# Gate values of the first chunk: four loads of each replaced by one load and a copy made by TensorE

## The chip, the cores and the metric

The kernel runs on one core of one Trainium2 chip. The metric is the device time of one execution in microseconds (us), and a kernel's time is the median of its runs. A profile is one execution recorded instruction by instruction; its span runs from the first to the last instruction of the program and is a little shorter than the device time.

## The reference

An mLSTM cell and a feed-forward layer follow each other. For each of 4 x 8 pairs of batch and head, over 768 tokens, with head size 40:

```python
m_new = max(f_gate[t] + m, i_gate[t])                 # m starts at -1e30
f_stab, i_stab = exp(f_gate[t] + m - m_new), exp(i_gate[t] - m_new)
C = f_stab * C + i_stab * outer(v[t], k[t]);  n = f_stab * n + i_stab * k[t]
y[t] = sigmoid(o_gate[t]) * (C @ q[t]) / max(abs(n . q[t]), 1)
```

The results are laid out as 3072 tokens of 320 values, x, and then `h = x @ w_in` (320 to 2048), `g = max(0.01 h, h)`, `out = g @ w_out` (2048 to 320). All of it is float32.

## The kernel before

**Tiling.** The sequence is cut into six chunks of 128 tokens. A step is one chunk of one batch, so there are 24 steps, and a chunk has four. Within a chunk the recurrence is written as a masked product: scores q.k are weighted by a matrix w of exponentials of gate sums, and the state carried from earlier chunks is added. The feed-forward layer of a chunk (`ff_units`) runs on TensorE between the cell work of the next chunk. TensorE, VectorE, ScalarE and GpSimd carry out their instructions in the order in which the program lists them (a hand-written order); each DMA queue (SyncE's, and ScalarE's for some loads) also issues in program order. A DMA takes one of eight completion semaphores, so its issue waits for the load that used that semaphore before it.

**Start of the program.** `first_chunk()` (L1169) is a hand-written list. SyncE's queue issues, in this order: the gate i loads, then k, q, v of step 0, k, q, v of step 1, the two o gates, and the first part of w_in; then the loads of steps 2 and 3 and the rest of w_in. ScalarE's queue issues the gate f loads and the gates of chunks 1 and 2.

**Gates of chunk 0.** `gates(0)` (L318) runs on VectorE over tiles f0 and i0, in which the 32 rows (batch and head) by 128 tokens stand four times over, on partitions 0-31, 32-63, 64-95 and 96-127: L109 to L111 load each of the two gates four times. F is the running sum of f (L325), m the running maximum (L329), `a = F - m` (L331) and `bu[:, 0] = i - F` (L333). For chunk 0 `a` lies in the third of three 128-column slots of `early`, an unused stretch of the later activations tile `acts`; the first two slots hold bf16 copies of the identity and of the causal mask, made by GpSimd (L152, L153).

**The spread.** `spread_masks()` (L475) writes the causal mask into four PSUM banks `ab` by four bf16 products of 512 columns (L479). `spread_first()` (L485) then adds a(t) + b(s) for every head: for each it multiplies a one-column pick from the identity, broadcast, with 32 rows of `a` or `bu` (L495). Four such products, one on each group of 32 rows of the array, run beside each other; this is why the gates stand on all four row groups. There are 32 products for `a` and 32 for `bu`, and the profile records each as two instructions. `first_exps()` (L500) turns the banks into w on ScalarE by four instructions (L504).

**What follows on TensorE.** `gates_T(0)` (L369) transposes the gate factors; `u_transpose(0)` (L629) transposes k and q of step 0 by eight products (L635), VectorE copies them out to kqT (L638); `u_scores(0)` (L640) multiplies them (L649) and VectorE multiplies the scores into w (L653). Step 1 follows in the same way, its kqT copied by ScalarE. `warm(6)` (L364, L367) is six products of the identity with itself, whose results nobody reads, issued ahead of the spread.

**After that.** `u_values`, `gate`, `u_x` and `state` finish steps 0 and 1; `narrow_weights` (L278 on) puts loaded weights into their final form on ScalarE (L300, L301) and VectorE (L302 to L309) as they land; L857 is the first feed-forward product. L413 and L522 are GpSimd's copies of v and mask additions for chunk 1, L621 the transposes of its k and q.

Of the kernel before, what the change touches and what calls it, by code (L numbers as in the profile page):

```python
# [9 lines left out]
F32 = mybir.dt.float32  # L10
# [9 lines left out]
def kernel(  # L20
# [26 lines left out]
    nc = tc.nc  # L47
    B, H, S, D = q.shape
    P = 128
    BH = B * H  # L50
# [16 lines left out]
    GT = B * P  # L67
# [13 lines left out]
    wk = ctx.enter_context(tc.tile_pool(name="wk", bufs=2))  # L81
    psf = ctx.enter_context(tc.tile_pool(name="psf", bufs=4, space=PSUM))
    psc = ctx.enter_context(tc.tile_pool(name="psc", bufs=4, space=PSUM))
# [18 lines left out]
    sync, by_act = queues = Ordered(nc.sync), Ordered(nc.scalar)  # L102

    RG = P // BH
    f_all = f_gate.rearrange("b h s -> (b h) s")
    i_all = i_gate.rearrange("b h s -> (b h) s")
    f0 = gp.tile([P, P], F32, name="f0")
    i0 = gp.tile([P, P], F32, name="i0")
    for r in range(RG):  # L109
        nc.scalar.dma_start(f0[ts(r, BH), :], f_all[:, :P])  # L110
        sync.dma_start(i0[ts(r, BH), :], i_all[:, :P])  # L111
    fi = {}

    def load_fi(c):
# [7 lines left out]
    ident = consts.tile([P, P], F32, name="ident")  # L122
# [24 lines left out]
    w_all = consts.tile([P, NL, H * P], F32, name="w")  # L147
    acts = consts.tile([P, NF, GT], F32, name="acts")
    acts_l = acts[:].rearrange("p f t -> p (f t)")
    early = acts_l[:, 5 * GT : 5 * GT + 3 * P].rearrange("p (n t) -> p n t", t=P)  # L150
    identb, cmaskb = (early[:, n, : P // 2].bitcast(BF16) for n in range(2))
    nc.gpsimd.tensor_copy(identb, ident[:])  # L152
    nc.gpsimd.tensor_copy(cmaskb, cmask[:])  # L153
    for n in range(NL):
        nc.vector.memset(kn[:, n, :, D:], 0.0)
        nc.vector.memset(qn[:, n, :, D:], 0.0)
        nc.gpsimd.memset(S_t[n][:, 1, :, D:], 2.0)
        nc.gpsimd.memset(S_t[n][SL:, 0], 0.0)
# [159 lines left out]
    def gates(c):  # L318


        m0 = m0s.get(c)
        n = P if c == 0 else BH
        fc, il = (f0[:], i0[:]) if c == 0 else (fi[c][:, 0, :], fi[c][:, 1, :])
        F = wk.tile([n, P], F32, name="F", bufs=1)
        nc.vector.tensor_tensor_scan(F[:], fc, zeros[:n].to_broadcast([n, P]), 0.0, op0=ALU.add, op1=ALU.add)  # L325
        if c > 0:
            nc.vector.tensor_scalar(il, il, scalar1=m0[:], scalar2=None, op0=ALU.subtract)
        m = wk.tile([n, P], F32, name="m", bufs=1)
        nc.vector.tensor_tensor_scan(m[:], fc, il, -1e30 if c == 0 else 0.0, op0=ALU.add, op1=ALU.max)  # L329
        a = early[:, 2, :] if c == 0 else wk.tile([n, P], F32, name="a", bufs=1)  # L330
        nc.vector.tensor_tensor(a[:], F[:], m[:], op=ALU.subtract)  # L331
        bu = wk.tile([n, 3, P], F32, name="bu", bufs=1)
        nc.vector.tensor_tensor(bu[:, 0, :], il, F[:], op=ALU.subtract)  # L333
        if c + 1 < NB:
            m1 = wk.tile([BH, 1], F32, name="m0")
            if c == 0:
                nc.vector.tensor_copy(m1[:], m[:BH, P - 1 :])
            else:
                nc.vector.tensor_tensor(m1[:], m0[:], m[:, P - 1 :], op=ALU.add)
            m0s[c + 1] = m1  # L340
        if c > 0:
            na = wk.tile([BH, 1], F32, name="na")
            nc.vector.tensor_tensor(na[:], m[:, SL - 1 : SL], F[:, SL - 1 : SL], op=ALU.subtract)
        bus[c] = bu, a, (na if c > 0 else None)
# [19 lines left out]
    def warm(n):  # L364
        t = psf.tile([P, P], F32, name="warm", tag="mm")
        for _ in range(n):
            nc.tensor.matmul(t[:], lhsT=ident[:], rhs=ident[:], start=True, stop=True)  # L367
# [47 lines left out]
    def load_first(s, i):  # L415

        d = st.setdefault(s, {})
        at = 4 * HW * 2 + s * Dm
        dst = (kn[:, s, :, :D], qn[:, s, :, :D], S_t[s][:, 1, :, :D], blocks(raw_l[:, at : at + Dm]))[i]
        d["k"], d["q"], d["va"], d["o"] = kn[:, s], qn[:, s], S_t[s][:, 1], raw_l[:, at : at + Dm]  # L420
        sync.dma_start(dst, (k, q, v, o_gate)[i][s, :, :P, :].rearrange("h p d -> p h d"))
# [43 lines left out]
    def spread_q(s):  # L465
# [4 lines left out]
        for r in range(2):  # L470
            sync.dma_start(
                d["ea"][ts(r, SL)], a_dr[c, 1, 1 - r, b * H : (b + 1) * H, :].partition_broadcast(SL),
            )

    def spread_masks():  # L475

        ab = [psf.tile([P, 2, H // RG, P], F32, name=f"ab{r}", tag="mm") for r in range(RG)]
        for t in ab:
            nc.tensor.matmul(  # L479
                t[:].rearrange("p n m t -> p (n m) t"), lhsT=identb,  # L480
                rhs=cmaskb.unsqueeze(1).to_broadcast([P, 2 * H // RG, P]), start=True, stop=False, skip_group_check=True,
            )
        return ab

    def spread_first(ab, a, bu, s2):  # L485

        for n in range(2):
            st.setdefault(s2 + n, {})["w"] = w_all[:, s2 + n].rearrange("p (h t) -> p h t", t=P)
            for m in range(H // RG):
                for left in (False, True)[: 1 if bu is None else 2]:  # L490
                    for r in range(RG):
                        bh = (s2 + n) * H + m * RG + r
                        rows = ts(r, BH)
                        pick = ident[rows, r * BH + bh : r * BH + bh + 1].to_broadcast([BH, P])
                        nc.tensor.matmul(  # L495
                            ab[r][:, n, m, :], lhsT=bu[rows, 0, :] if left else pick, rhs=pick if left else a[rows, :],
                            start=False, stop=left or bu is None, skip_group_check=True,
                        )

# [129 lines left out]
    def u_transpose(s, copies):  # L629
        d = st[s]  # L630
        d["kqT"] = wk.tile([P, 2, PR * P], F32, name="kqT")
        for i in range(2):
            tp = psc.tile([P, PR, P], F32, name="tkq", tag="c")
            for j in range(PR):
                nc.tensor.transpose(  # L635
                    tp[:, j, :], d["kq"[i]][:, 2 * j : 2 * j + 2, :].rearrange("p h d -> p (h d)"), ident[:],
                )
            copies[i](d["kqT"][:, i], tp[:].rearrange("p j t -> p (j t)"))  # L638
# [530 lines left out]
    def first_chunk():  # L1169

        for n in range(2):
            for i in range(3):
                load_first(n, i)
        for n in range(2):
            load_first(n, 3)
        load_weights(0, (0,))
        on_v, on_s = nc.vector.tensor_copy, nc.scalar.copy
        gates(0)
        gates_exp(0)
        load_fi(2)  # L1180
        warm(6)
        ab = spread_masks()
        bu, a, _ = bus[0]
        spread_first(ab, a, bu, 0)
        gates_T(0, bu)
        prep_vu(0)
        first_exps(ab, 0)
        u_transpose(0, (on_v, on_v))
        u_scores(0)
        u_transpose(1, (on_s, on_s))  # L1190
        ab = spread_masks()
        gates(1)
        u_scores(1)
        prep_vu(1)
        prepare_tiles()
        e = next_exps(ab, 2)
        w, w1 = narrow_weights(0, 0), narrow_weights(0, 1)
        n0, n1 = narrow_weights(1, 0), narrow_weights(1, 1)
        ffs = []
        prep_o(0)  # L1200
        prep_o(1)
        u_values(0)
        gate(0)
        spread_first(ab, a, None, 2)
        u_values(1)
        load_first(2, 0)
        load_first(2, 1)
        load_weights(0, (1,))
        load_first(3, 0)
        load_first(3, 1)  # L1210
        load_first(2, 2)
        load_first(3, 2)
        load_first(2, 3)
        load_first(3, 3)
        load_weights(1, (0,))
        load_weights(1, (1,))
        run(e, 6)
        u_x(0)
        gate(1)
        run(w, 2)  # L1220
        run(w, 4)
        u_x(1)
        state(0)
        state(1)
        state_copy(0)
        state_copy(1)
        prepare_step(0)
        prepare_step(1)
        run(e, 2)
        ffs = ff_units(0)  # L1230
        u_transpose(2, (on_s, on_s))
        run(e, 4)
        gates_exp(1)
        run(w1, 2)
        run(e, 4)
        ffs[0]()
        run(w1, 2)
        prep_vu(2)
        prep_vu(3)
        u_scores(2)  # L1240
        u_transpose(3, (on_v, on_s))
        run(w1, 2)
        u_gates(1)
        u_scores(3)
        prep_o(2)
        prep_o(3)
        u_values(2)
        ffs[1]()
        gate(2)
        u_values(3)  # L1250
        gate(3)
        u_x(2)
        state(2)
        u_x(3)
        state(3)
        state_copy(2)
        run(n0, 4)
        state_copy(3)
        run(n0, 2)
        run(n1, 6)  # L1260
        prepare_step(2)
        prepare_step(3)
        return ffs
# [160 lines left out]
```

## Time and profile before

| | us |
|---|---|
| device time, median of 3 runs (lowest to highest) | 476.22 (475.19 to 476.83) |
| span of the profiled execution | 472.6 |
| TensorE matmul busy | 462.6 |
| VectorE / ScalarE / GpSimd busy | 339.1 / 203.7 / 172.0 |

The device time of the profiled execution alone is not given; its span lies 3.6 us below the median of the runs. In the rows of the profile, PE is TensorE's matmul side and PEld its weight loads, DVE is VectorE, ACT ScalarE, POOL GpSimd, SP SyncE; a q behind a name (SPq, ACTq) is that engine's instruction queue, where DMAs are issued. A row of the timeline has start, duration, engine, source line, operation, out<-in, shapes and count, and in brackets how long the engine had been idle and what ended that. Neighbouring instructions of one kind are merged into one row, and rows of one engine can overlap, since products are pipelined.

### The profile page before, as it was taken

What the parts mean: (1) busy time and instruction counts of PE and PEld (TensorE: products, weight loads), DVE (VectorE), ACT (ScalarE), POOL (GpSimd) and SP (SyncE); (2) the same over time, 40 slices, a digit from 0 to 9 for tenths busy, and PEclk for the clock granted to TensorE, in tenths of its full rate; (3) what the DMA queues carried; (4) which work ended last, traced back from release to release, by engine and by line L of the source; (5) the groups of instructions that cost most, each with busy time, mean ns of one, the idle gap of its engine ahead of it and who ended that gap; (6) DMA issues with size and microseconds to landing.
All of it is one profiled execution on the core that took longest, in us unless ns stands there. A gap on an engine that the chain in (4) does not pass through costs nothing.

```text
span 472.6 us, 14150 instructions
## 1 busy us (share of the span) xinstructions
PE 462.6 (98%) x5729; PEld 417.8 (88%) x5729; DVE 339.1 (72%) x607; ACT 203.7 (43%) x497; POOL 172.0 (36%) x205
## 2 busy tenths in 40 slices
PE   7998999999999999999999999999999999999997
PEld 6787878777788899988999988999988999988997
DVE  3878589999579989878688867788947786105531
ACT  3755888755336511367311366311456311253210
POOL 4340577264335164923214923214822005300020
PEclk9999999999999999999999999999999999999999
DMA  9999988877742594865755764853875203100001
GB/s 117 174 176 183 223 192 229 199 154 159 155 135 56 157 171 107 185 152 115 179 125 108 172 144 120 196 120 76 189 147 122 65 21 81 58 0 2 8 8 42
DMA packets 161281, 59.31 MB, mean 126 GB/s; under 512 B 123904, under 2 KB 152640, under 8 KB 161216
## 3 DMA queue, kind: packets, MB, share of 16 engines
q1 hardware_dynamic: 121088, 51.20, 49.0%
q10 hardware_dynamic: 40128, 7.21, 9.3%
q8 instruction: 45, 0.74, 0.7%
q14 instruction: 20, 0.16, 0.2%
HBM read 51.68 MB, written 6.70 MB: 124 GB/s over the span
## 4 chain that ended last, share of the span: by engine, by line
PE 86%; SPq 6%; DMA 3%; DVE 1%; ACT 1%; issue 1%; POOL 0%; DVEq 0%; ACTq 0%
PE ph L1021 33%; PE po L914 33%; PE po L879 8%; SPq L96 6%; PE pT L796 3%; PE sd L708 3%; PE ph L857 3%; DMA acts<-in_moe_w_in_dram 2%; DMA acts<-in_v_dram 1%; PE sd L714 1%; PE hN L768 1%; PE tk L621 0%; ACT kqT L627 0%; PE tq L606 0%; DVE w_in L308 0%
## 5 line engine op out<-in xcount | busy, mean ns | idle before, releaser
L914 PE MATMUL po<-w_out,acts 128*128 128x160 f32 x640 | 89.1, 300 | 0.0
L914 PEld LDWEIGHTS po<-w_out,acts 128*128 128x128 f32 x640 | 87.3, 190 | 0.6 <-ACT acts L1046 0.3
L1021 PE MATMUL ph<-xT,w_in 64*128 64x256 f32 x720 | 82.7, 378 | 0.0
L1021 PEld LDWEIGHTS ph<-xT,w_in 64*128 64x128 f32 x720 | 69.5, 187 | 8.3 <-issue 0.6
L1050 DVE TENSOR_TENSOR acts<-acts,ph 128x512 f32<-128x512 f32 x60 | 38.4, 682 | 40.4 <-PE ph L1021 40.3
L914 PE MATMUL po<-raw,acts 128*128 128x160 f32 x480 | 66.4, 300 | 0.0
L914 PEld LDWEIGHTS po<-raw,acts 128*128 128x128 f32 x480 | 65.4, 190 | 0.3
L1054 ACT COPY acts<-ph 128x512 f32<-128x512 f32 x60 | 32.2, 588 | 49.5 <-PE ph L1021 49.5
L522 POOL TENSOR_TENSOR w<-w,i 128x512 f32<-128x512 f32 x20 | 31.9, 1603 | 53.2 <-DMA w<-a_dr 22.1
L1046 ACT ACTIVATE acts<-acts 128x1024 f32<-128x1024 f32 x30 | 31.6, 1055 | 40.6 <-DVE acts L1050 32.3
L684 POOL TENSOR_TENSOR S<-S,f 40x336 f32<-40x336 f32 x36 | 31.3, 868 | 46.7 <-PE pT L796 31.1
L530 ACT ACTIVATE w<-w,gT 128x64 f32<-128x64 f32 x160 | 41.6, 337 | 12.3 <-DMA a_dr<-a 5.3
L725 DVE TENSOR_TENSOR qn<-w,sd 64x384 f32<-64x384 f32 (+1 forms) x80 | 33.4, 418 | 13.7 <-ACT acts L1054 7.8
L857 PE MATMUL ph<-xT,w_in 64*128 64x256 f32 x320 | 37.9, 383 | 1.8 <-DVE w_in L309 0.7
L879 PE MATMUL po<-w_out,acts 128*128 128x320 f32 x128 | 36.7, 437 | 0.0
L857 PEld LDWEIGHTS ph<-xT,w_in 64*128 64x128 f32 x320 | 31.5, 187 | 5.8 <-ACT acts L865 1.1
L810 POOL TENSOR_TENSOR xb<-xb,den 128x320 f32<-128x320 f32 x16 | 11.6, 727 | 67.7 <-DVE xb L807 65.4
L1021 PE MATMUL ph<-acts,w 64*128 64x256 f32 x320 | 36.3, 379 | 0.0
L1021 PEld LDWEIGHTS ph<-acts,w 64*128 64x128 f32 x320 | 30.6, 187 | 3.6
L879 PEld LDWEIGHTS po<-w_out,acts 128*128 128x128 f32 x128 | 23.5, 190 | 9.2 <-ACT acts L865 0.3
L595 DVE TENSOR_TENSOR qn<-kqT,ea 64x512 f32<-64x512 f32 x32 | 30.9, 965 | 0.8
L952 POOL TENSOR_TENSOR y<-y,raw 128x160 f32<-128x160 f32 x10 | 9.5, 953 | 59.2 <-ACT y L951 59.2
(181 smaller groups left out, 736.5 us busy)
## 6 DMA issues: line engine op xcount, KB each, us to landing
rb<-in_k_dram SPq DMA_DIRECT2D x64, 80.0 KB
rb<-in_q_dram SPq DMA_DIRECT2D x64, 80.0 KB
rb<-in_o_gate_dram SPq DMA_DIRECT2D x64, 80.0 KB
ea<-a_dr SPq DMA_DIRECT2D x32, 128.0 KB
raw<-in_moe_w_out_dram SPq DMA_DIRECT2D x6, 640.0 KB
w<-a_dr ACTq DMA_DIRECT2D x24, 128.0 KB
x_dr<-x SPq DMA_DIRECT2D x64, 40.0 KB
xT<-x_dr SPq DMA_DIRECT2D x16, 160.0 KB
```

The costliest lines, as they stand in the source:

```text
L522: nc.gpsimd.tensor_tensor(w, w, cm2.unsqueeze(1).to_broadcast([P, H, SL]), op=ALU.add)
L530: yield nc.scalar.activation(w[:, h, :], w[:, h, :], AF.Exp, bias=gT[c][:, 0, bh : bh + 1], scale=1.0)
L595: nc.vector.tensor_tensor(mixed(s)[rows, 1 - r], d["kqT"][rows, 1].rearrange("p (h t) -> p h t", t=SL), d["ea"][rows], op=ALU.mult,)
L684: nc.gpsimd.tensor_tensor(new, old, g, op=ALU.mult)
L725: nc.vector.tensor_tensor(mixed(s)[toks, u, hs], w[toks, hs], bank[1 - u][to[u][hs.start], hs], op=ALU.mult,)
L857: nc.tensor.matmul(ph[r][:, cols], lhsT=w_row(r, slot, j), rhs=xT[DP * r : DP * (r + 1), slot, cols], start=(slot == 0), stop=(slot == KC ...
L879: nc.tensor.matmul(po[n][:], lhsT=acts[:, f, ts(n, P)], rhs=w_out[:, f, :], start=(f == 0), stop=(f == NF - 1),)
L914: nc.tensor.matmul(bank[:], lhsT=left[:, f, :], rhs=right[:, f, :], start=f == 0, stop=f == KH - 1)
L1021: nc.tensor.matmul(bank[r][:, e, :], lhsT=left(r)[rows, e], rhs=right(r)[rows], start=first and e == 0 and m == 0, stop=e == 1 and m == le ...
L1046: nc.scalar.activation(to, z, AF.Prelu, alpha=0.01)
L1050: nc.vector.tensor_tensor(to[:, 2 * r : 2 * r + 2], to[:, 2 * r : 2 * r + 2], bank[r], op=ALU.add)
L1054: nc.scalar.copy(to[:, 2 * r : 2 * r + 2], bank[r])
```

## The change

Each gate of chunk 0 is loaded once, onto partitions 0-31, and `gates(0)` works on 32 rows. GpSimd makes one more tile in `early` (now four slots): on 32 rows, the 32-by-32 identity four times side by side. A new function, `replicate`, multiplies it with `a` and with `bu[:, 0]` on TensorE, which puts both on four row groups in PSUM; one VectorE copy of 128 x 256 brings them to SBUF, where the spread reads them. `u_transpose(0)` moves from behind `first_exps` to ahead of the spread. `warm(6)` becomes `warm(2)`. The second spread, for steps 2 and 3, reads the same copied `a`.

```diff
-    for r in range(RG):
-        nc.scalar.dma_start(f0[ts(r, BH), :], f_all[:, :P])
-        sync.dma_start(i0[ts(r, BH), :], i_all[:, :P])
+    nc.scalar.dma_start(f0[:BH], f_all[:, :P])
+    sync.dma_start(i0[:BH], i_all[:, :P])
...
-    early = acts_l[:, 5 * GT : 5 * GT + 3 * P].rearrange("p (n t) -> p n t", t=P)
+    early = acts_l[:, 5 * GT : 6 * GT].rearrange("p (n t) -> p n t", t=P)
...
     nc.gpsimd.tensor_copy(cmaskb, cmask[:])
+    nc.gpsimd.tensor_copy(early[:BH, 2, :].rearrange("p (r n) -> p r n", r=RG), ident[:BH, :BH].unsqueeze(1).to_broadcast([BH, RG, BH]))
...
-        n = P if c == 0 else BH
-        fc, il = (f0[:], i0[:]) if c == 0 else (fi[c][:, 0, :], fi[c][:, 1, :])
+        n = BH
+        fc, il = (f0[:BH], i0[:BH]) if c == 0 else (fi[c][:, 0, :], fi[c][:, 1, :])
...
-        a = early[:, 2, :] if c == 0 else wk.tile([n, P], F32, name="a", bufs=1)
+        a = wk.tile([n, P], F32, name="a", bufs=1)
...
+    def replicate(a, bu):
+        rows = early[:, 2:]
+        t = psc.tile([P, 2, P], F32, name="rep", tag="c")
+        pick = rows[:BH, 0, :]
+        for n, part in enumerate((a[:], bu[:, 0, :])):
+            nc.tensor.matmul(t[:, n, :], lhsT=pick, rhs=part, start=True, stop=True)
+        nc.vector.tensor_copy(rows, t[:])
+        return rows[:, 0, :], rows[:, 1, :]
...
-                            ab[r][:, n, m, :], lhsT=bu[rows, 0, :] if left else pick, rhs=pick if left else a[rows, :],
+                            ab[r][:, n, m, :], lhsT=bu[rows, :] if left else pick, rhs=pick if left else a[rows, :],
...
-        warm(6)
+        warm(2)
         ab = spread_masks()
         bu, a, _ = bus[0]
-        spread_first(ab, a, bu, 0)
+        a, left = replicate(a, bu)
+        u_transpose(0, (on_v, on_v))
+        spread_first(ab, a, left, 0)
         gates_T(0, bu)
         prep_vu(0)
         first_exps(ab, 0)
-        u_transpose(0, (on_v, on_v))
         u_scores(0)
```

More of the change, by code (lines that the diff above doesn't have):

```diff
@@ L336, in gates @@
             if c == 0:
-                nc.vector.tensor_copy(m1[:], m[:BH, P - 1 :])
+                nc.vector.tensor_copy(m1[:], m[:, P - 1 :])
             else:
```

## The prediction

> **What bounds the kernel now.** I read the page's slices first, then TensorE's busy time in stretches of the start, then the waits there, then the chain of waits. The slices:
>
> ```profile
> PE   7998999999999999999999999999999999999997
> DMA  9999988877742594865755764853875203100001
> ```
>
> TensorE is below nine tenths only in the first slices and the last one; the DMA engines are full in the first five slices, 59 us. Two stretches ahead of 70 us and one behind (start:end, length, then busy time and instruction count of PE, PEld, DVE, ACT, POOL; DMA share and GB/s at the end):
>
> ```profile
> 45.00:50.00 5.00, 3.95 (x91) 3.58 (x93) 4.73 (x12) 4.55 (x8) 2.84 (x3) 1.00 0.83 192
> 65.00:70.00 5.00, 4.04 (x90) 3.31 (x90) 4.86 (x6) 4.93 (x15) 4.78 (x6) 1.00 0.73 174
> 70.00:75.00 5.00, 5.00 (x91) 4.35 (x81) 4.69 (x9) 4.62 (x11) 3.73 (x5) 1.00 0.82 216
> ```
>
> The slices have TensorE full from there to the last one, so this change can be worth only what it takes off the time at which TensorE gets there. What holds it up before that are loads, as the timeline shows:
>
> ```profile
> 42.46 0.78 ACT L865 ACTIVATE acts<-ph 128x256 f32<-128x256 f32 x2 [1.37 <-PE ph L857]
> 45.42 0.80 ACT L300 ACTIVATE w_in<-raw 128x640 f32<-128x640 f32 x1 [2.17 <-DMA raw<-in_moe_w_in_dram]
> 52.41 4.86 PE L857 MATMUL ph<-xT,w_in 64*128 64x256 f32 x40 [0.73 <-ACT acts L865]
> 60.93 1.79 POOL L522 TENSOR_TENSOR w<-w,i 128x512 f32<-128x512 f32 x1 [7.27 <-DMA w<-a_dr]
> ```
>
> ScalarE waits 2.17 us for w_in at 45.42 and is then busy (4.55 of 5 us to 50, all but the end of that wait) until it releases TensorE at 52.41; GpSimd waits 7.27 us for w at 60.93, and TensorE's last gap, between 65 and 70 us, comes behind that. The chain of waits (start, duration, what) follows the first of these loads back through SyncE's queue to the issue of the first big one:
>
> ```profile
> 2.58 0.42 SPq L96
> ...
> 28.96 8.66 DMA acts<-in_moe_w_in_dram
> 37.73 0.80 ACT w_in L300
> ```
>
> So the start is a train of loads in one queue. Its time is when the first big load is issued, plus work that keeps the DMA engines full.
>
> **The change part by part.**
>
> *The loads.* The queue's start now:
>
> ```profile
> 0.75 1.79 SPq L96 DMA_DIRECT2D i<-in_i_gate_dram  x4
> 0.76 1.84 ACTq L110 DMA_DIRECT2D f<-in_f_gate_dram  x4
> 2.58 0.42 SPq L96 DMA_DIRECT2D kn<-in_k_dram  x1
> 3.05 0.58 SPq L96 DMA_DIRECT2D qn<-in_q_dram  x1
> 6.39 1.30 SPq L96 DMA_DIRECT2D S<-in_v_dram  x1
> ```
>
> Three of SyncE's four gate issues go: (2.58 - 0.75) x 3/4 = 1.37 us. k of step 0 is issued at 1.21, and every load behind it moves with it, since by the program nothing in that queue waits for arithmetic in the first 30 us: an issue waits for the load eight before it, and that moves too. ScalarE's own loads, of the gates of chunk 1, move by as much. The six loads also leave the DMA engines. For the first 10 us ScalarE's queue, eight loads of 16 KB, shows the first of these rows (packets, MB, share of 16 engines); the others are stretches:
>
> ```profile
> q10 hardware_dynamic: 384, 0.13, 6.9%
> 1.00:2.00 1.00, 0.53 (x2) 0.53 (x3) 1.00 (x6) 0.00 (x0) 0.96 (x5) 1.00 0.09 26
> 3.00:4.00 1.00, 1.00 (x7) 1.00 (x7) 0.00 (x0) 0.33 (x1) 0.89 (x3) 1.00 0.38 71
> 6.00:7.00 1.00, 1.00 (x17) 0.97 (x20) 0.00 (x0) 0.00 (x0) 0.00 (x0) 1.00 1.53 146
> ```
>
> 0.69 us of all engines, so six loads are 0.5. That is the upper bound of what their absence adds; nothing is the lower, since before 4 us the share is 0.09 to 0.38 against 1.53 when full (shares add up overlapping packets). I take 0.1, near the lower end.
>
> *The gates on 32 rows.* VectorE starts at 4.03, 1.43 us after the last of ScalarE's issues ended (0.76 + 1.84 = 2.60):
>
> ```profile
> 4.03 0.42 DVE L325 TENSOR_TENSOR_SCAN F<-f,zeros 128x128 f32<-128x128 f32 x1 [1.47 <-DMA f<-in_f_gate_dram]
> 13.34 0.41 DVE L325 TENSOR_TENSOR_SCAN F<-fi,zeros 32x128 f32<-32x128 f32 x1
> 5.01 0.28 DVE L333 TENSOR_TENSOR bu<-i,F 128x128 f32<-128x128 f32 x1
> 1.47 2.93 PE L367 MATMUL warm<-ident 128*128 128x128 f32 x12 [1.47 <-POOL ident masks.py:199]
> 4.19 1.91 PE L479 MATMUL ab<-acts 128*128 128x512 bf16 x4
> ```
>
> One issue ends at 1.22, so F starts at 2.65; 32 rows cost what 128 do (0.41 against 0.42). bu was done 5.29 - 4.03 = 1.26 after the start, so a and bu stand at 3.9, not 5.3.
>
> *Two idle products for six.* Twelve records in 2.93 us are 0.24 each; two products end at 2.45, and the four mask products, 1.91, at 4.36. TensorE waits for nothing there: its masks are made ahead of GpSimd's added copy. That copy, 32 x 128, delays only the clearing of tiles that are used later; its price lies between nothing and the 0.72 us of GpSimd's 128 x 320 product (row at 11.96 below), and GpSimd's next work waits for gT, at 9.04, anyway.
>
> *The copy onto four row groups.* Two products are four records at 0.24: 4.36 to 5.34. Then VectorE's 128 x 256 copy out of PSUM; no row has this shape, and the bounds are these two:
>
> ```profile
> 9.04 0.22 DVE L380 COPY gT<-tg 128x64 f32<-128x64 f32 x1 [3.69 <-PE tg L373]
> 9.53 1.29 DVE L638 COPY kqT<-tkq 128x512 f32<-128x512 f32 x2 [0.26 <-PE tkq L635]
> ```
>
> 0.22 to 0.65; by columns 0.4. Below the first it cannot be. It lies beside TensorE's transposes of step 0, and costs nothing there; without them it would be 0.4 on the path.
>
> *The transposes ahead of the spread.* TensorE takes its instructions in order, so the spread, and behind it the exponentials, now wait until k and q of step 0 have landed and eight transposes are through. Rows:
>
> ```profile
> 6.03 0.81 PE L495 MATMUL ab<-acts,ident 32*128 32x128 f32 x8
> 6.62 0.65 PE L495 MATMUL ab<-ident,bu 32*128 32x128 f32 x8
> 7.05 0.65 PE L495 MATMUL ab<-acts,ident 32*128 32x128 f32 x8
> 7.76 0.39 PE L495 MATMUL ab<-acts,ident 32*128 32x128 f32 x8
> 7.98 0.39 PE L495 MATMUL ab<-ident,bu 32*128 32x128 f32 x8
> 8.85 2.06 ACT L504 ACTIVATE w<-ab 128x512 f32<-128x512 f32 x4 [3.12 <-PE tg L373]
> 11.96 0.72 POOL L540 TENSOR_TENSOR vu<-S,gT 128x320 f32<-128x320 f32 x1 [1.64 <-DMA S<-in_v_dram]
> 12.13 1.28 DVE L653 TENSOR_TENSOR w<-w,sc 128x512 f32<-128x512 f32 x2 [1.32 <-PE sc L649]
> 12.66 1.07 ACT L638 COPY kqT<-tkq 128x512 f32<-128x512 f32 x2 [1.75 <-PE tkq L635]
> ```
>
> The groups of the spread begin 0.43 us apart (6.62, 7.05) and later 0.22 (7.76, 7.98): TensorE goes from half speed to full near 7.5, though the view's granted clock says 1.00 there. At half speed eight transposes at 0.24 last from 5.34 to 7.3. The landing of q has no row; bounds: the gate's load took 1.43 + 0.46 = 1.9 us from its issue, v of step 1, with the queue full, 11.96 - 6.39 = 5.6. Issued at 1.68, q lands between 3.6 and 7.3; by its place, second of six, near 5. TensorE wants it at 6.3; at the late bound the spread comes 1 us later. So the spread starts at 7.3, not 6.03, has one slow group and seven fast, and ends at 9.3, not 8.65: 0.6 late. The exponentials run from 9.45 to 11.5. But the eight transposes behind the spread are gone, and kqT is copied long before: scores run from 9.5 to 10.6, VectorE starts on w when the third exponential ends, 9.45 + 1.55 = 11.0, not 12.13, and ScalarE copies step 1's kqT at 11.5, not 12.66. Arithmetic is **1.1 us earlier** from there. GpSimd's scaling of v, behind gT, comes some 0.6 later than now; only the state products at the end of steps 0 and 1 read it.
>
> **Sum.** Loads 1.37 + 0.1, arithmetic 1.1 earlier. ScalarE was free at 43.25 and waited until 45.42, so for its gain the loads decide, and they pass 1.47 on to 52.41 and, through the w load at 60.93, to 70. The span becomes 472.6 - 1.5 = 471.1. The median of the runs shown lies 3.6 above the profiled span; with the same 3.6 the time is **474.7**, 0.32% less.
>
> **The rivals.**
>
> *Arithmetic comes late* (ends above). With loads 1.37 earlier ScalarE's free time ahead of 45.42 is 2.17 - 1.37 = 0.8 us, if arithmetic has not moved. If it is x us later than now, the gain is 1.37 - (x - 0.8): nothing at x = 2.17, a loss beyond. The mechanism is half speed on TensorE that lasts longer because four idle products are gone and the products are fewer. If it lasts until step 1's scores are done (now at 15.0): the spread takes 7.3 to 10.75. Step 1's scores follow in the trace at
>
> ```profile
> 10.87 1.16 PE L649 MATMUL sc<-kqT 40*128 40x128 f32 x16 [0.94 <-DVE kqT L638]
> 13.85 1.16 PE L649 MATMUL sc<-kqT 40*128 40x128 f32 x16
> ```
>
> From the spread's end at 8.65 to 15.0 are 6.35 us, less the 0.94 idle and 1.0 of step 0's transposes 4.4 of work; at half speed 8.8, so the scores end at 19.5, x = 4.5, and the loss is 2.3: **478.5**. It decides where half speed lasts beyond about 15 us (x = 2.17). Against it: TensorE is as continuously busy as now, from 1.47 to 9.3. For it: the slow state is seen to last 6 us after the first product. The Trainium skill's "TensorE: Matmul & The Clock Gate", Part 1, says that the array runs at half rate until about 3.4 us of a free-running window have been busy, since the default is the throttled state; this speaks against taking products out. By that rule idle products at the start buy full speed. The trace agrees on two speeds, groups 0.43 and 0.22 apart. By the page's figure one window more would end at an estimated 10.9, and the spread's slow groups would then cost about 1.5 us: x = 0.4, within ScalarE's 0.8, and the sum would stay.
>
> *Arithmetic takes part of the gain*: q lands late or the clock rises late, x between 1 and 2: gains of 1.2 to 0.2, about **475.5**.
>
> *The change does not do what it says*: the DMA engines, not the issues, pace the first loads, so that issuing earlier moves nothing, **476.2**. Against it: the shares of 0.09 to 0.38 above.
>
> **How the numbers follow.** I give the forecast 0.73; late arithmetic 0.14; partial 0.08; nothing 0.05. The forecast's own range is 473.6 to 475.6: 0.5 more for the six loads' DMA time, 0.9 less if waits further on give some back, and the 0.4 or so by which runs differ. A change of 0.3%, 1.43 us, is about what a measurement of this kernel tells from none; the forecast lies just beyond it (474.79), so of its 0.73 I give 0.52 to faster and 0.21 to within. The partial case and the one of nothing are within; of the late one 0.12 is slower, 0.02 within. Faster 0.52, within 0.36, slower 0.12. The range 473.5 to 477.0 holds forecast, partial and nothing and leaves out most of the late case.
>
> **What would show it.** SyncE issues k at 1.2; ScalarE's waits at 37.7 and 45.4 end 1.4 earlier; TensorE starts its product at 51.0, not 52.41; VectorE's first w product starts near 11.0; the spread near 7.3, with groups 0.22 apart soon after. Groups still 0.43 apart at the end of the spread would point to the clock; a spread held beyond 7.5 by a wait for q, to the load; waits at 45.4 that have not moved, to DMA engines that set the pace. The forecast is wrong, too, if TensorE has new gaps after 70.

## The result and the profile after

The changed kernel takes **474.30 us** (median of 18 runs, 472.69 to 475.71) against 475.47 (18 runs, 474.52 to 477.68) for the kernel before. The ratio is 0.997 with a 95% interval of 0.9959 to 0.998: faster, by about as much as the 0.3% that was taken as the bound of what can be told. 474.7 had been predicted.

Two corrections of the scale come first. With 18 runs the median of before is 475.47, not the 476.22 of the first three. And every run of the changed kernel lists its device time 1.8 us above its span (474.27 and 472.5 in the profiled one). The span of 472.6 shown of before thus belongs to a run of about 474.4, one of its quickest. The two profiled spans, 472.6 and 472.5, differ by nothing; the medians differ by 1.17. So where the gain lies has to be read stage by stage.

The slices of the changed kernel (page, part 2):

```profile
PE   8999989999999999999999999999999999999997
DMA  9999978878752695865755765753774203100001
```

TensorE still has its low slices ahead of 70 us only. Three stretches, with the same columns as those shown of before:

```profile
45.00:50.00 5.00, 5.00 (x102) 4.51 (x104) 4.73 (x11) 4.91 (x12) 4.58 (x5) 1.00 0.94 195
65.00:70.00 5.00, 3.76 (x116) 3.02 (x114) 4.79 (x5) 4.89 (x17) 4.25 (x5) 1.00 0.56 148
70.00:75.00 5.00, 5.00 (x77) 4.26 (x77) 4.71 (x9) 4.04 (x10) 2.48 (x5) 1.00 0.73 193
```

TensorE is busy for all of 45 to 50 us, where it was for 3.95 of 5. The gap between 65 and 70 is still there. What TensorE waited for between 20 and 72 us, first before, then after (us in all, times, longest):

```profile
PE tk L621 <- DMA kn<-in_k_dram: 1.1, 1, 1.1
PE sd L714 <- POOL vu L550: 1.0, 1, 1.0
PE ph L857 <- DVE w_in L309: 0.7, 1, 0.7
PE ph L857 <- ACT acts L865: 0.7, 1, 0.7
PE xt L845 <- DVE x L756: 0.5, 1, 0.5
PE ph L857 <- DVE S L672: 0.4, 1, 0.4
```

```profile
PE sd L724 <- POOL vu L560: 1.1, 1, 1.1
PE ph L867 <- DVE w_in L309: 0.8, 1, 0.8
PE xt L855 <- DVE x L766: 0.5, 1, 0.5
PE tg L373 <- DVE w L663: 0.3, 1, 0.3
```

4.4 us before, 2.7 after: the waits for k of a later step, for ScalarE at 52.41 and for the state are gone. (Lines of the program are 10 higher behind the new function.) The rows that answer to those of the prediction, in the order of the timeline:

```profile
43.14 0.80 ACT L300 ACTIVATE w_in<-raw 128x640 f32<-128x640 f32 x1
...
45.94 9.31 PE L867 MATMUL ph<-xT,w_in 64*128 64x256 f32 x80
...
60.43 1.27 POOL L532 TENSOR_TENSOR w<-w,i 128x512 f32<-128x512 f32 x1 [8.73 <-DMA w<-a_dr]
```

ScalarE begins on w_in at 43.14 with no wait at all, where it waited 2.17 us until 45.42. TensorE's product, which had been cut at 52.41, runs from 45.94 to 55.25 in one piece, about 2 us earlier. GpSimd's mask addition at 60 is only 0.5 earlier. The start:

```profile
1.20 0.42 SPq L96 DMA_DIRECT2D kn<-in_k_dram  x1
1.67 0.57 SPq L96 DMA_DIRECT2D qn<-in_q_dram  x1
...
2.72 0.41 DVE L325 TENSOR_TENSOR_SCAN F<-f,zeros 32x128 f32<-32x128 f32 x1 [0.16 <-DMA f<-in_f_gate_dram]
...
7.38 0.81 PE L505 MATMUL ab<-acts,ident 32*128 32x128 f32 x8
7.97 0.65 PE L505 MATMUL ab<-ident,acts 32*128 32x128 f32 x8
...
9.67 0.65 PE L505 MATMUL ab<-ident,acts 32*128 32x128 f32 x8
10.10 0.47 PE L505 MATMUL ab<-acts,ident 32*128 32x128 f32 x8
10.40 0.39 PE L505 MATMUL ab<-ident,acts 32*128 32x128 f32 x8
...
12.43 1.28 DVE L663 TENSOR_TENSOR w<-w,sc 128x512 f32<-128x512 f32 x2 [1.19 <-ACT w L514]
...
12.74 1.11 ACT L648 COPY kqT<-tkq 128x512 f32<-128x512 f32 x2
```

k is issued at 1.20, as forecast, and the spread starts at 7.38, as forecast. But its groups stay 0.43 us apart until 10.10, where one slow group and seven quick ones were forecast: TensorE came to full speed near 10.2. So VectorE reaches w at 12.43 and ScalarE kqT at 12.74, where 11.0 and 11.5 were forecast and 12.13 and 12.66 stood before: the 1.1 us of arithmetic did not come. The page also has TensorE busy for 464.3 us, 1.7 more than before, though it has four idle products less. Of that the start, with the slow groups, has 0.9 (18.48 us busy in the first 20 against 17.58); the rest lies behind.

How the two spans come out equal is seen on ScalarE. The same instruction starts at 51.97 before and at 49.96 after, a later one at 75.25 and 73.93, then at 149.09 and 148.99, and at 284.71 and 284.69. In this execution 2.0 us were won by 50 us and given back between 52 and 150, far behind the slow groups. In a second execution of the changed kernel (d4 below) the same four start at 49.86, 74.21, 148.14 and 283.60: there 1.1 us of 2.1 are kept to the end. One pair of profiles doesn't show the gain; the medians do.

### The profile page after: what moved, and what is told of

Same layout as the page of the kernel before. It is cut to its first block, busy times and chain, and to the rows that moved or that the text cites. A ratio compares the mean times of both kernels' runs of the same rounds, so it can differ in the third digit from the quotient of the medians.

```text
span 472.5 us, 14135 instructions
## 1 busy us (share of the span) xinstructions
PE 464.3 (98%) x5725; PEld 417.9 (88%) x5725; DVE 341.8 (72%) x608; ACT 203.3 (43%) x497; POOL 169.5 (36%) x206
## 4 chain that ended last, share of the span: by engine, by line
PE 80%; SPq 9%; DVE 4%; DMA 2%; ACT 2%; POOL 2%; issue 1%; DVEq 0%; ACTq 0%; POOLq 0%
PE ph L1031 33%; PE po L924 33%; SPq L96 9%; PE po L889 4%; PE pT L806 3%; PE sd L718 3%; PE ph L867 1%; DMA w<-a_dr 1%; PE sd L724 1%; DVE qn L735 1%; DVE w_out L309 1%; DMA raw<-in_o_gate_dram 1%; DVE w_out L308 1%; DVE w_out L302 1%; PE hN L778 0%
## 5 line engine op out<-in xcount | busy, mean ns | idle before, releaser
L532 POOL TENSOR_TENSOR w<-w,i 128x512 f32<-128x512 f32 x20 | 30.6, 1539 | 55.5 <-DMA w<-a_dr 40.0
L867 PE MATMUL ph<-xT,w_in 64*128 64x256 f32 x320 | 37.7, 383 | 0.8 <-DVE w_in L309 0.8
```

The costliest lines, as they stand in the source:

```text
L532: nc.gpsimd.tensor_tensor(w, w, cm2.unsqueeze(1).to_broadcast([P, H, SL]), op=ALU.add)
L867: nc.tensor.matmul(ph[r][:, cols], lhsT=w_row(r, slot, j), rhs=xT[DP * r : DP * (r + 1), slot, cols], start=(slot == 0), stop=(slot == KC ...
```

## The experiments

Theory L: the train of loads sets the time, and issuing it 1.37 us earlier is the whole gain. Rivals: the transposes ahead of the spread or the earlier arithmetic make it; or the DMA engines pace the train and something else does. A second question was the clock. All ratios are to the kernel before, run in turn with each set; the median of before differs by 1.2 us between the sets, so ratios and medians are compared inside a set (the e, the d and the f runs). d4 and f2 are the changed kernel itself, unchanged, as the measure inside their sets. Times expected in us were reckoned from a kernel before of 475.5; in the set of the e runs it takes 476.48, so these are read as ratios.

| run | median | before | ratio (95%) |
|---|---|---|---|
| e1_loads_back | 476.65 | 476.48 | 1.0003 (0.9982 to 1.0024) |
| e2_loads_alone | 474.66 | 476.48 | 0.9973 (0.9952 to 0.9994) |
| e3_six_idle | 475.39 | 476.48 | 0.9985 (0.9962 to 1.0007) |
| e4_transposes_back | 475.01 | 476.48 | 0.9975 (0.9958 to 0.9993) |
| d1_six_more | 477.40 | 476.71 | 1.0008 (0.9992 to 1.0025) |
| d2_gate_by_scalar | 474.67 | 476.71 | 0.9950 (0.9928 to 0.9972) |
| d3_late_scores | 475.94 | 476.71 | 0.9975 (0.9959 to 0.9992) |
| d4_same_again | 474.82 | 476.71 | 0.9966 (0.9951 to 0.9982) |
| f1_q_by_scalar | 474.30 | 475.62 | 0.9970 (0.9950 to 0.9990) |
| f2_third_look | 474.70 | 475.62 | 0.9977 (0.9961 to 0.9994) |
| f3_gate_by_scalar | 474.53 | 475.62 | 0.9969 (0.9955 to 0.9984) |
| f4_later_scores | 481.26 | 475.62 | 1.0118 (1.0099 to 1.0138) |

### The loads put back, and the loads alone

```diff
+    for r in range(1, RG):                                  # e1
+        nc.scalar.dma_start(f0[ts(r, BH), :], f_all[:, :P])
+        sync.dma_start(i0[ts(r, BH), :], i_all[:, :P])
```

> The changed kernel with the six removed gate loads issued again, three on each queue behind the one that stays; what they bring is read by nobody, everything else is as changed. Theory (the train of loads): k of step 0 is issued 1.37 us later, near 2.57, every load behind it with it, TensorE's gaps near 40, 45 and 52 us come back, and the time goes back to the kernel before, 475.5 us (475.1 to 475.9), ratio 1.000. Rival (the gain comes from the transposes ahead of the spread, and the loads were hidden anyway): 474.3, as in the changed kernel.

Measured: 1.0003, 476.65 us. The gain is gone. ScalarE's and SyncE's rows:

```profile
2.59 0.43 SPq L96 DMA_DIRECT2D kn<-in_k_dram  x1
...
45.74 0.80 ACT L303 ACTIVATE w_in<-raw 128x640 f32<-128x640 f32 x1 [1.40 <-DMA raw<-in_moe_w_in_dram]
```

k at 2.59 and the w_in wait ending at 45.74 are those of before (2.58 and 45.42). In this run arithmetic was also late, since TensorE, with the transposes ahead of the spread, waited 0.38 and 0.26 us for k and q and came to full speed only behind the spread; but ScalarE's wait for the load is there all the same.

```diff
-        warm(2)                                             # e2: all three edits, e3: the first, e4: the other two
+        warm(6)
...
-        u_transpose(0, (on_v, on_v))
         spread_first(ab, a, left, 0)
...
         first_exps(ab, 0)
+        u_transpose(0, (on_v, on_v))
         u_scores(0)
```

> The changed kernel with six idle products and with the transposes of step 0 back behind the exponentials: what stays of the change are the single loads and the copy onto four row groups by TensorE. Theory (the train of loads): 474.3 us, all of the gain (474.0 to 474.7). Rival (the early transposes make the gain): 475.5.

Measured: 0.9973, 474.66 us: nearly 2 us under e1 in the same set, and all of the gain, with the old order and six idle products. Its interval and that of e1 still overlap (0.9982 to 0.9994), but ten of its twelve runs lie below the quickest of e1's twelve (475.99). The single loads make the gain.

> The changed kernel with six idle products at its start in place of two. If idle products at the start bring the full clock sooner, the groups of the spread are 0.22 us apart from about 8 us on, and the exponentials start near 9.5 to 10 in place of 10.8; if not, the four products (1.0 us of TensorE) only delay the copy and all behind it, and the exponentials start near 11.5. The time, by the theory of the loads, does not move either way, 474.3 us (474.0 to 474.6), since ScalarE has 2.2 us before the load of w_in that it waits for; by the rival (arithmetic counts) it moves with the exponentials, to about 473.3 or 475.

Measured: 0.9985, 475.39 us. This is the run in which the arithmetic did come early, as the forecast had wanted it:

```profile
6.91 0.50 PE L505 MATMUL ab<-acts,ident 32*128 32x128 f32 x8
7.23 0.40 PE L505 MATMUL ab<-ident,acts 32*128 32x128 f32 x8
...
8.57 0.40 PE L505 MATMUL ab<-ident,acts 32*128 32x128 f32 x8
```

```profile
8.99 2.06 ACT L514 ACTIVATE w<-ab 128x512 f32<-128x512 f32 x4 [4.68 <-PE tg L373]
...
44.26 0.80 ACT L300 ACTIVATE w_in<-raw 128x640 f32<-128x640 f32 x1 [1.99 <-DMA raw<-in_moe_w_in_dram]
```

TensorE is at full speed from before the spread, the exponentials start 1.8 us earlier than in the changed kernel, and ScalarE waits those 2 us away again at 44.26. The median is no better than that of e2 (474.66), so early arithmetic shows no gain. It is known for this one execution only, though, which at 473.31 us is 2.1 under the median of its run, and the interval holds no change as well as the whole gain.

> The changed kernel with the transposes of step 0 back behind the exponentials, two idle products kept. TensorE then waits about 0.4 us for VectorE's copy onto four row groups ahead of the spread, and the spread starts near 5.9. If the full clock comes some time after the first product whatever TensorE does, it comes at 10.2 again and the spread, all of it at half speed, ends near 9.4. The time by the theory of the loads: 474.3 us (474.0 to 474.7); by the rival that the early transposes make the gain: 475.5.

Measured: 0.9975, 475.01 us. The time is, by its ratio, as expected; the clock is not:

```profile
4.72 0.38 PE L481 MATMUL rep<-bu,acts 32*128 32x128 f32 x2
...
5.69 0.50 PE L505 MATMUL ab<-acts,ident 32*128 32x128 f32 x8 [0.59 <-DVE acts L482]
6.01 0.40 PE L505 MATMUL ab<-ident,acts 32*128 32x128 f32 x8
6.24 0.40 PE L505 MATMUL ab<-acts,ident 32*128 32x128 f32 x8
```

Groups 0.22 apart from 6 us on, with two idle products and the same first 4.3 us of TensorE as in the changed kernel, where they were 0.43 apart until 10.1. TensorE was at full speed before 5 us: the products that copy bu take 0.38 here, and 0.63 (from 4.92) in the changed kernel. In this execution two idle products were enough; whether six make it likelier is taken up under the clock. The copy onto four row groups costs TensorE 0.59 here, with no transposes to hide it (0.4 was priced).

### The clock

> The changed kernel once more, unchanged, for the clock. If the time at which TensorE comes to full speed is a property of the kernel, the groups of the spread are 0.43 us apart until about 10 again. If it hangs on where a free-running window stands when the program starts, as the Trainium skill's TensorE: Matmul & The Clock Gate, Part 1, states, it comes at another time within some 3.4 us of the first profile's, and the first exponential starts anywhere from about 9 to 11. By either the time is that of the changed kernel, ratio 0.997.

Measured: 0.9966; full speed between 9.2 and 9.6, and the first exponential at 10.43:

```profile
9.24 0.49 PE L505 MATMUL ab<-acts,ident 32*128 32x128 f32 x8
9.57 0.39 PE L505 MATMUL ab<-ident,acts 32*128 32x128 f32 x8
```

> The changed kernel, unchanged, beside the three others of this set: ratio 0.997 to the kernel before. Its first exponential shows the time of full speed a third time: by the theory of the free-running window it starts somewhere between about 9 and 11.5, by the theory that the kernel sets it, at 10.4 to 10.8 as in the two profiles so far.

Measured: 0.9977; the groups close up at 9.08 and the first exponential is at 10.17. So one kernel came to full speed at 10.2, 9.3 and 8.9 in three executions, and e4, the same up to 4.3 us, did before 5: the time differs from execution to execution. The Trainium skill's "TensorE: Matmul & The Clock Gate", Part 1, states this, a free-running window of 3.4 us whose place differs from run to run; the trace agrees that it varies. It puts the variation at about half a microsecond in one place; here it is 1.3 us within one program, and over 3 with e4.

That the program has no part in it isn't shown, and the profiles lean the other way. All three with six idle products are at full speed by about 7.5 us: before, e2 (its products that copy a take 0.48 from 5.86, against 0.79 in the changed kernel) and e3 (its four mask products take 1.13 from 4.19, against 1.91). Of the eleven with two, e4 and d1 are before 5, and the other nine only at 8.9 or later. Three executions against eleven don't settle it, and what makes a window count as busy was not tried.

The third execution holds one thing more. Two stretches of f2, with TensorE's busy time first; of the last three columns the first is the granted clock, the share of full speed that TensorE was given:

```profile
60.00:63.40 3.40, 1.18 (x38) 0.97 (x35) 1.45 (x6) 0.61 (x2) 0.51 (x1) 1.00 0.56 78
63.50:66.90 3.40, 3.40 (x68) 2.98 (x67) 0.90 (x2) 1.62 (x3) 3.12 (x6) 0.50 1.10 273
```

And what lies ahead of the second:

```profile
63.38 0.25 PE L631 MATMUL tk<-ident,rb 64*40 64x64 f32 x2 [2.22 <-DMA rb<-in_q_dram]
```

A load of q of a later step landed late, TensorE waited 2.22 us, and right behind the wait its clock was granted at 0.50 for 3.4 us, in which it was busy throughout; from 66.9 on it is 1.00 again. So 3.4 x 0.5 = 1.7 us of full speed are gone on top of the wait. The span of f2 is 474.4, that of d4, the same kernel, 471.3; in d4 the clock is 1.00 from 60 to 70 us. One kernel has a wait of 2.22 us with a slow clock behind it in one execution, and of 0.7 in another: this is one way in which runs of one kernel come to differ by 3 us, and why a gain of 1.4 is hard to see in two profiles.

### More and fewer issues

```diff
+    for r in range(1, RG):                                  # d1
+        sync.dma_start(f0[ts(r, BH), :], f_all[:, :P])
+        sync.dma_start(i0[ts(r, BH), :], i_all[:, :P])
```

> The changed kernel with six gate loads more in SyncE's queue, between i and k of step 0; what they bring is read by nobody. At 0.45 us an issue, k is issued 2.7 us later than in the changed kernel and 1.35 later than before. Theory (the train of loads decides, one for one): 1.2 us over the kernel before plus what the six take of the DMA engines, ratio 1.003 (1.002 to 1.005). Rival (loads decide only within a slack of about 1.4 us, beyond it something else): ratio 1.000.

Measured: 1.0008, 477.40 us. Against the unchanged copy of this set (0.9966) six issues, 2.77 us (k at 3.97), cost 0.0042, 2.0 us by the ratios and 2.6 by the medians. The interval holds the lower end of what theory L expects (1.002 to 1.0025) and the rival's 1.000 too. Ten of the twelve runs of d4 lie below the quickest of d1 (475.80), so more issues do cost time. One for one fits the first 1.4 us (e1); beyond, this run doesn't settle it, since in its profile the loads don't decide alone. TensorE waited 2.03 us for k of step 0 and 0.64 for q. It had been at full speed ahead of that (the products that copy bu take 0.38 from 4.80); then its clock was granted at half:

```profile
8.10:18.30 10.20, 9.79 (x97) 8.45 (x98) 4.04 (x11) 3.52 (x8) 3.27 (x10) 0.50 1.38 168
```

That is 10.2 x 0.5 = 5.1 us of full speed, and ScalarE comes to the load of w_in at 47.72 without a wait: by then arithmetic was later than the train.

```diff
-    sync.dma_start(i0[:BH], i_all[:, :P])                   # d2, f3
+    nc.scalar.dma_start(i0[:BH], i_all[:, :P])
```

> The changed kernel with the single load of gate i issued by ScalarE's queue, behind f; SyncE's queue starts with k of step 0. k is issued at 0.75 in place of 1.20, and gate i lands about 0.45 us later, as VectorE's scan of m begins. Theory (train of loads): 0.45 us less than the changed kernel, ratio 0.996 to the kernel before (0.994 to 0.998). Rival (beyond the 1.4 us won, arithmetic decides): as the changed kernel, 0.997.

> Once more the changed kernel with gate i issued by ScalarE's queue behind f, to settle whether it is ahead of the changed kernel. In its first profile k was issued 0.45 us earlier, but gate i landed at 5.55 in place of 2.46, behind k and q, and all arithmetic came 1.8 us later. Theory (loads alone decide): 0.9955, some 0.4 us under the changed kernel of this set. Rival (the late arithmetic takes it back): 0.997 or above.

Measured: 0.9950 and 0.9969, against 0.9966 and 0.9977 of the copies of the changed kernel in the same sets. Both below, neither beyond its interval. The gate came late in both, behind k and q:

```profile
5.58 0.41 DVE L329 TENSOR_TENSOR_SCAN m<-f,i 32x128 f32<-32x128 f32 x1 [1.74 <-DMA i<-in_i_gate_dram]
```

VectorE's scan of m starts at 5.58 (d2; 5.07 in f3) instead of 3.06, and the first exponential is 1.8 us later than in d4 and f2. With k issued 0.45 us earlier, the time doesn't rise. Whether it falls by the 0.45 that theory L expects, these intervals can't tell.

```diff
-            for i in range(3): load_first(n, i)             # f1, step 0
+        load_first(0, 0); load_first(0, 1, nc.scalar); load_fi(1); load_first(0, 2)
```

> The changed kernel with q of step 0 issued by ScalarE's queue, right behind gate f and ahead of the gates of chunk 1; SyncE's queue goes from k of step 0 straight to v. q is issued at 1.22 in place of 1.67, v of step 0 at 1.67 in place of 2.29, gate i stays first in its queue. Theory (the train of loads): 0.4 to 0.6 us less than the changed kernel, ratio 0.9955 (0.994 to 0.998) to the kernel before. Rival (from 2 us on the DMA engines and no longer the issues pace the train): as the changed kernel, 0.997.

Measured: 0.9970, against 0.9977: 0.3 us, which fits theory L (0.994 to 0.998) and the rival alike. The rows speak for the rival. SyncE issued the second k at 2.28 instead of 3.08 (f2), but the q behind it took 2.24 us to issue instead of 1.13, and the v behind that was issued at 5.36 instead of 5.09: the lead was gone. In the changed kernel the issues ahead of 3 us take 0.40 to 0.67 us each and the next three 0.93 to 1.12. That transfers hold the issues from there on is read from these rows; no run tries it by itself. No version beats the changed kernel beyond doubt.

### Late arithmetic

```diff
-        for _ in range(3 if s == 3 else 0):                 # d3; f4 with 36
+        for _ in range({0: 18, 3: 3}.get(s, 0)):
```

> The changed kernel with 18 idle products more on TensorE ahead of the scores of step 0: at 0.11 us for each of their two records at full speed, all arithmetic from there on is about 4 us later; the loads stay. Theory of the prediction (ScalarE has some 2 us before the w_in load that it waits for; what is later than that counts): about 2 us over the changed kernel, ratio 1.001 to 1.003 to the kernel before. Rival A (loads alone decide, the slack is larger than 4 us): 0.997. Rival B (no slack at all, every microsecond of arithmetic counts): ratio 1.005 to 1.006.

Measured: 0.9975, against 0.9966 of d4: 0.4 us by the ratios, 1.1 by the medians. That is rival A's number; the 1.001 to 1.003 of the prediction's slack lies outside the interval.

```profile
10.30 4.29 PE L655 MATMUL sc<-ident 128*128 128x128 f32 x36
```

The scores start at 14.52, so TensorE has 4.22 us more to do. Its waits from 20 to 72 us, of d4 and then of d3:

```profile
PE sd L724 <- POOL vu L560: 1.1, 1, 1.1
PE ph L867 <- DVE w_in L309: 0.8, 1, 0.8
PE tk L631 <- DMA rb<-in_q_dram: 0.7, 1, 0.7
PE xt L855 <- DVE x L766: 0.5, 1, 0.5
PE ph L867 <- ACT acts L875: 0.2, 1, 0.2
```

```profile
PE ph L867 <- DVE w_in L309: 0.8, 1, 0.8
PE xt L855 <- DVE x L766: 0.5, 1, 0.5
PE sd L724 <- POOL vu L560: 0.3, 1, 0.3
```

The extra work filled waits: 3.3 us became 1.6, and none that stays names a load. In these two executions the spans differ by 2.6 us (473.9 and 471.3), about what the waits don't cover of 4.22; but d4's is the quickest of its twelve.

> The changed kernel with 36 idle products ahead of the scores of step 0, twice as many as in the earlier run: arithmetic some 8 us later, loads as they are. In the second profile of the changed kernel the waits that late arithmetic can fill add up to 2.8 us: 0.85 of ScalarE at 43.3, and 0.21, 0.67 and 1.06 of TensorE at 50, 61 and 68. If these are the whole cover, the time is 5.2 us over the changed kernel, ratio 1.008 (1.005 to 1.010) to the kernel before. If the prediction's 0.8 us are, 1.012. If loads decide whatever arithmetic does, 0.997 to 1.000.

Measured: 1.0118, 481.26 us: 6.6 over f2, for 8.2 us of work. All waits for loads are gone, and new ones have come:

```profile
30.45 1.30 DVE L309 CUSTOM_DVE_ANT_0 w_in<-acts,w_in 128x1280 uint16<-128x1280 uint16 x1
...
31.80 1.57 PE L867 MATMUL ph<-xT,w_in 64*128 64x256 f32 x12 [1.72 <-DVE w_in L309]
```

VectorE's L309, begun while GpSimd was scaling v (from 30.34), lasts 1.30 us where d3's took 0.82, and TensorE waits 1.72 for it instead of 0.75. So the number is that of the prediction's slack (1.012), but the way is not: waits taken away and waits added. From d3 and f4 the cover is between 1.6 us (8.2 less 6.6) and 3.8 (4.2 less 0.4); closer it isn't settled.

## Why the prediction was right, point by point

**What bounds the kernel.** Right. A train of loads sets when TensorE gets to 70 us: put back (e1), the gain goes; alone (e2), it stays.

**The loads, 1.37 + 0.1.** Right in mechanism and nearly in size. k went from 2.58 to 1.20; w_in's wait at 45.42 vanished; the ratio of 0.997 is 1.4 us, the medians give 1.17. The load itself moves less evenly than the queue's head: where ScalarE waits for it, it lands between 43.28 (f1) and 44.30 (e2) with single loads, against 45.42 and 45.74 (e1) with all eight, so 1.1 to 2.5 us earlier. The wait at 37.7 was to end 1.4 earlier, too; it vanished, but ScalarE came to that load no earlier (37.72 against 37.73). What the six loads take of the DMA engines could not be told from nothing.

**Arithmetic 1.1 earlier.** Wrong in this kernel's profile: +0.3 and +0.1 us instead (12.43 and 12.74). The step that failed is "TensorE goes from half speed to full near 7.5", read off one execution and taken for the program's. The place differs between executions (8.9 to 10.2 for this kernel). The prediction had weighed one window more and put its end at 10.9; that case came, at 10.2, and as the prediction said of it, the sum stayed: arithmetic 1.8 us earlier (e3) shows no gain, 1.8 us later (d2, f3) no loss.

**Where the copy lies, the prices of the parts.** Right: F at 2.72 (2.65 forecast), spread at 7.38 (7.3), VectorE's copy 0.42 us (0.4) beside the transposes.

**"Passed on through the w load at 60.93, to 70".** Half right. TensorE was 2 us ahead at 55, but the w load landed only 0.5 earlier, and GpSimd's chain kept TensorE's wait of 1.1 us between 65 and 70. At 75 us 1.3 of the 2.0 are left, and 1.0 of 2.1 in d4. In this execution more was given back further on:

```profile
100.00:105.00 5.00, 4.62 (x21) 2.98 (x21) 4.88 (x9) 0.48 (x2) 2.09 (x3) 1.00 0.52 105
130.00:135.00 5.00, 4.65 (x152) 3.69 (x150) 2.80 (x7) 1.07 (x2) 2.94 (x3) 1.00 0.69 156
```

Two new gaps, 0.38 and 0.35 us, in stretches that were full before. In d4 and e3 TensorE is full from 72 to 400 us, in d3, f1 and f2 a gap of 0.3 to 0.4 stands between 105 and 135; of the kernel before there is one profile. They differ between executions; whether the change makes them likelier stays open, and so does where the other 0.6 of the 1.3 went. "New gaps after 70" as a sign of a wrong forecast was too sharp.

**The scale, 472.6 + 3.6.** Wrong: the offset is 1.8, and 3.6 came from a quick execution held against three slower runs. Base and sum shared the error, so the difference was hardly touched: 1.5 forecast, 1.2 to 1.4 measured. That 474.7 itself lies only 0.4 above the 474.30 is in part luck: the base of 476.22 was 0.75 above the later 475.47.

**The rivals.** Late arithmetic with its price of 1.37 - (x - 0.8) counted only ScalarE's free time; behind it lie TensorE's waits at 61 and 68, and the cover is 1.6 to 3.8, not 0.8. It would decide later than x = 2.17: d3 is some 4 us late and still under the kernel before. "The DMA engines pace the first loads" is wrong for the 1.37 us taken here; for what goes beyond, the issue rows of f1 speak for it, while the times of d2, f1 and f3 can't tell the 0.4 us in question from nothing.

## What to carry to other kernels

Where a train of loads in one queue ends the last wait, small loads at its head cost their issue, 0.45 us each here, and duplicates that TensorE can copy belong out of it; but, by the rows of f1, only until the issues themselves grow long, here from about 3 us. Work in front of a wait for that train is free within its cover, and earlier work showed no gain. A time at which the clock rises, read from one execution, is not a property of the kernel; look at a second execution of the same program before pricing by it, and before reading a difference of 1 us out of two profiles.

## What was not expected of the hardware

The time of full speed moved between under 5 us (e4, d1) and 10.2 us, and in e1 beyond 11.9, among executions whose TensorE work was the same up to 4.3 us. A wait of 2.22 us in the middle of the program was followed by a granted clock of 0.50 for 3.4 us, though TensorE was busy throughout, and that one execution was 3.1 us longer than another of the same kernel. In d1 a wait of 2.03 us, to 7.21, was followed by 0.50 from 8.1 to 18.3. Gate i, a load of 16 KB, landed in time for 3.06 when it was issued first in its queue at 0.75, and held VectorE until 5.58 (d2; 5.07 in f3) when it was issued at 1.25 behind k and q on the other queue: half a microsecond of issue became at least 2 of landing. And VectorE's L309 took 0.82 us in d3 and 1.30 in f4, where GpSimd had begun its own work first.
